# Batch 0's queries by parity of heads, landmarks of two batches ahead: a fused two-step attention and feed-forward kernel

## The chip, the core and the metric

The kernel runs on one core of a Trainium2 chip. A core has a matrix engine (TensorE, PE in the profile; its weight loads are PEld), a vector engine (VectorE, DVE), an engine for pointwise functions (ScalarE, ACT), GpSimd (POOL) and SyncE (SP). Each works through its own instructions in order and waits for the others on semaphores. Loads and stores are issued by SP and ACT (HWDGE, descriptors made in hardware) and by POOL (SWDGE, descriptors made by software, which can cast on the way); all share 16 DMA engines. The metric is the device time of one execution in microseconds, the median of several runs. The result is compared with a float32 reference.

## The reference

Eight batches of eight heads, 576 positions, width 64, with 32 landmarks p per head:

```
p_packed = softmax(scale * p k^T) v          # 32 x 64 per head
a        = softmax(scale * q p_packed^T) p_packed
x        = a, heads side by side             # 4608 tokens x 512
h        = x w_in                            # 4608 x 2048
g        = h if h >= 1;  0 if h <= -1;  (h + 1)^2 / 4 between
out      = g w_out                           # 4608 x 512
```

## The kernel before, in words

The kernel never forms x. For each batch it computes M = p_packed w_in (per head, so 8 x 32 = 256 rows by 2048 columns, kept as two groups g of 128 rows) and the normalized second softmax A (the same 256 rows by 576 tokens); then h = M^T A. Heads are paired: head 2a + g lies in group g, so group 0 has the even heads and group 1 the odd ones.

The stages of a batch, with their lines: turning the landmarks (`landmarks`, L321 on PE into tpp, copied by L189 into pT); turning k and q (`turned`, L362 into tp, copied into kT and qT); scores sp (L413) and their exponential ex (L419); p_packed and its row sums pk (L445, L450), copied into ppT, with reciprocals rs (L462); second scores s (L472, function `probs`, s2 in the code), exponential eT (L482), column sums sm (L487), logarithm ln (L491) and exponential rc (L495) for the reciprocal, product A (L500 on DVE); M (L528 into mp, in four slices f of 512 columns, each needing one slice of w_in, copied into M). Then 16 hidden blocks fi: h (L562, four products each), x (L567, ACT), t (L572 on DVE or L574 on ACT), hT (L579, DVE). The output (L619) is taken for pairs of batches in nine row blocks i of 128 tokens, each summing the 16 blocks fi; it needs w_out's slice fi // 4. L189 is the helper `copy`, through which all copies go.

The instructions are not in the order of the program text. Each step is added to a planner (`Plan`) with a rank, its duration on each engine that may do it, what it depends on and the buffers it takes. The planner runs through time with its own costs, picks for each engine the step of lowest rank among those that can start first, and so fixes engine and order; the program is then emitted in that order. The planner's ranks for batch 0's blocks, batch 1's stages and the first output blocks are the constants PITCH0, T1, L1, M1, KT1, QT1, SC1, ST1, MT1 and EARLY (start and length for each output block); LENT names output blocks of the first pair that take their accumulator from pool w instead of pool o. Pool w has three PSUM buffers, which serve every stage but the outputs; pool o has two.

Until the first output, PE's gaps are filled with products of zeros (L687, `warm`), as many as the planner's gaps hold; they keep PE active and compute nothing.

The loads go out by POOL in the order of the string LOADS (k0 is k of batch 0; heads 0 to 3 of it come by SP and ACT through k_raw, and the landmarks of batch 0 through p_raw, ahead of it on the same two queues). Batch 0's q comes in three parts of heads: 0 to 3, 4 and 5, 6 and 7. The landmarks of batches 1 to 7 (p) come by POOL behind k1. From batch 3 on, k and q are turned by DMA.

Of the kernel before, what the change touches and what calls it, by code (L numbers as in the profile page):

```python
# [116 lines left out]
def kernel(  # L117
# [35 lines left out]
    FIRST = 3  # L153
    LOADS = "k0 v0 q0 win0 win1 win2 wout0 win3 wout1 k1 p wout2 v1 wout3 q1 k2 q2 v2"
    H1, H2 = 20.58, 43.17
    PITCH0, PITCH1 = 1.03, 0.66
    T1, T2 = 3.46, 22.00
    LENT = [1, 4]
    L1, M1 = 11.28, 4.03
    KT1, QT1 = 7.75, 9.42  # L160
    SC1, PK1 = 10.26, 9.59
    ST1, MT1 = 12.34, 16.34
    EARLY = [[(3.62, 21.4), (13.89, 9.61), (23.95, 3.31), (31.73, 16.65)], [(26.33, 7.57), (43.04, 6.63), (54.6, 5.54), (55.23, 18.49), (62.39, 4.68)]]

# [31 lines left out]
    def either(dve, act, *pairs, parted=None):  # L196

        def emit(e):
            for to, of in pairs:
                copy(e, to(), of(), parted)  # L200
        return {"DVE": (dve[0], dve[1], emit), "ACT": (act[0], act[1], emit)}


    p_raw = const.tile([NP, H, D], f32, name="p_raw")
    p_nat = const.tile([NP, B, H, D], bf16)
# [12 lines left out]
    def constants(e):  # L218
        V.memset(zeros, 0.0)  # L219
        V.memset(pT[:, 0].rearrange("p g a x n -> p (g a x n)"), 0.0)  # L220
# [6 lines left out]
    consts = plan.add(-1000, {"DVE": (2.2, 2.2, constants)})  # L227

# [27 lines left out]
    def rows_of(nm, b, h0, h1):  # L256
        return {"k": k, "q": q, "v": v}[nm][b, h0:h1].rearrange("h (p c) d -> p h (c d)", c=NC)

    def load(nm, b, rank):

        parts = {("k", 0): [4, 8], ("q", 0): [0, 4, 6, 8]}.get((nm, b), [0, 8])
        for i, (h0, h1) in enumerate(zip(parts, parts[1:])):
            def emit(e, h0=h0, h1=h1):
                G_.dma_start(tokens(nm, b)[:, h0:h1], rows_of(nm, b, h0, h1))  # L264
            mb = MB0.get((nm, b, h0), 1.18 * (h1 - h0) / H)
            t = dma((nm, b, h0), rank + 0.01 * i, emit, mb, [nm] if i == 0 else [], 0.9 if b < FIRST else 3.0)
            for h in range(h0, h1):
                landed[nm, b, h] = [t]
# [8 lines left out]
    def load_p(rank):  # L277
        dma("p", rank, lambda e: G_.dma_start(p_nat[:, 1:].rearrange("n b h d -> n (b h) d"),
                                              p[1:].rearrange("b h n d -> n (b h) d")), 0.6)

# [13 lines left out]
    def load_p_raw(e):  # L294
        for i, queue in enumerate((nc.sync, nc.scalar)):
            queue.dma_start(p_raw[:, 4 * i:4 * i + 4], p[0, 4 * i:4 * i + 4].rearrange("h n d -> n h d"))

    p_first = plan.add(-1000, {"SP": (1.0, 3.3, load_p_raw)})

    def load_k_raw(e):  # L300
        for i, queue in enumerate((nc.sync, nc.scalar)):
            queue.dma_start(k_raw[:, 2 * i:2 * i + 2], rows_of("k", 0, 2 * i, 2 * i + 2))

# [32 lines left out]

    p_cast = plan.add(-900, {"DVE": (0.41, 0.41, lambda e: V.tensor_copy(p_nat[:, 0], p_raw))}, [p_first])
    landmarks(0, 1, -900, [p_cast, identity])

    A_of, M_of, rs_of = {}, {}, {}  # L340

    def attention(b, at, fine):

        ready = {}

        def turned(nm, h0, h1):

            n = h1 - h0
            rank = at[nm + "T"] + 0.075 * h0
            banks = [(0, (0, 2)), (1, (2, 3))] if n == 4 else [(j, (0, E)) for j in range(n)]  # L350

            def place(tp, j, c):
                return tp[:, 0, (j * 2 + c) * TP:][:, :TP] if n == 4 and c < 2 else \
                    tp[:, 1, j * TP:][:, :TP] if n == 4 else tp[:, j, c * TP:][:, :TP]

            def turn(e):
                if h0 == 0:
                    have[nm + "T", b] = new(nm + "T", [P, H, E, TP], bf16)
                have["tp" + nm, b, h0] = tp = wide([P, 2, 1024], bf16, "tp")
                for c in range(E):  # L360
                    for j in range(n):
                        nc.tensor.transpose(place(tp, j, c),  # L362
                                            have[nm, b][:, h0 + j, X * c:X * (c + 1)].rearrange("p c d -> p (c d)"),
                                            ident[:TP, :TP])

            t = plan.add(rank, {"PE": (0.51 * n / 4, 0.17 + 0.51 * n / 4, turn)}, landed[nm, b, h0] + [identity],
                         ["w"] + ([nm + "T"] if h0 == 0 else []), behind=[ready.get((nm, "turn"))])
            ready[nm, "turn"] = t
            ev = []
            for y, (c0, c1) in banks:  # L370
                to = lambda y=y, c0=c0, c1=c1: (have[nm + "T", b][:, h0:h1, c0:c1] if n == 4 else
                                                have[nm + "T", b][:, h0 + y])
# [8 lines left out]
            for h in range(h0, h1):  # L381
                ready[nm, h] = ev
            return t
# [13 lines left out]
        for nm in "kq":  # L397
            parts = [0, 4, 6, 8] if (nm, b) == ("q", 0) else [0, 4, 8]
            users[nm] = [turned(nm, *p) for p in zip(parts, parts[1:])] if b < FIRST else crossed(nm)
            plan.release(nm, users[nm])  # L400
# [29 lines left out]
        if b == 0:  # L430
            have["others"] = plan.add(-27, {"DVE": (1.56, 1.56, lambda e: V.memset(
                pT[:, 1:].rearrange("p b g a x n -> p (b g a x n)"), 0.0))}, [consts], behind=ready["k", 4])

# [31 lines left out]

        def probs(e):
            for g in range(G):
                have["s2", b, g] = s2 = wide([P, X, FW], f32, "s2")
                for a in range(Q):
                    for x in range(X):  # L470
                        r = slice(x * D, (x + 1) * D)
                        nc.tensor.matmul(s2[a * NP:(a + 1) * NP, x, :HALF], have["ppT", b][r, g, a],  # L472
                                         have["qT", b][r, G * a + g].rearrange("p e t -> p (e t)"),
                                         start=True, stop=True)

        s2 = plan.add(at["s2"], {"PE": (0.32, 0.47, probs)}, pp + list({id(t): t for h in range(H) for t in ready["q", h]}.values()), ["w", "w", "eT", "eT"], mode="s")
        plan.release("qT", [s2])
        before = None
        for g in range(G):
# [23 lines left out]
            r = at["sm"] + 0.2 * g  # L503
            t_e = plan.add(r, {"ACT": (0.68, 0.745, exp)}, [s2, rs])
            plan.release("w", [t_e])
# [13 lines left out]
        for fs in groups:  # L519
# [28 lines left out]
        plan.release("ppT", mms + [s2])  # L548

# [173 lines left out]
```

## Time and profile before

| | |
|---|---|
| median of 3 runs | 250.58 us (250.34 to 250.84) |
| the profiled execution | 250.97 us |
| its span, first to last instruction | 249.1 us |
| PE busy | 243.0 us, 98% of the span |
| ACT busy | 196.7 us, 79% |
| DVE busy | 176.6 us, 71% |
| filling products (L687) | 48, busy 13.5 us |
| loads and stores | 34.67 MB |

A row of the order of time gives start, duration, engine, line, operation, output and inputs, how often it stands there merged, and in brackets how long the engine had been idle and what ended that. The engine named is the one whose semaphore came last by the profile; where that engine had long been done, it was another, often a load. Rows of one engine overlap a little at their ends, since instructions are pipelined: four h products follow each other at shorter distance than the duration shown for each.

### The profile page before, as it was taken

The page shows a single profiled execution, that of the slowest core. Times are in us where ns is not written, and L with a number is a line of the kernel's source. Part 1 is how long each engine was busy: PE and PEld are TensorE (multiplying, and loading weights), DVE is VectorE, ACT ScalarE, POOL GpSimd, SP SyncE. Part 2 cuts the span into 40 slices and gives each one's busy share as a digit, 9 for nine tenths or more (in the row PEclk, how much of TensorE's full clock was granted, in tenths as well). Part 3 has the DMA queues.
Part 4 walks back from the last instruction along what each step waited for, and adds up shares of the span by engine and source line. Part 5 has one row for each costly group of instructions (what it writes and reads, how often), then busy time and mean ns, then how long its engine had stood idle before and what let it go on. Part 6 is the DMA issues. An engine that isn't in the chain of part 4 may idle for free.

```text
span 249.1 us, 5894 instructions
## 1 busy us (share of the span) xinstructions
PE 243.0 (98%) x2416; PEld 138.7 (56%) x2416; DVE 176.6 (71%) x295; ACT 196.7 (79%) x327; POOL 27.9 (11%) x41
## 2 busy tenths in 40 slices
PE   8999999999999999999999999999999999999994
PEld 3644665576645646645565455655565555555453
DVE  4548997679868999979966777679686776776000
ACT  4587986899799999899978977799968977886111
POOL 8542110211003000400030003000000000000000
PEclk9999999999999999999999999999999999999999
DMA  7999999999999949896999689995111111112223
GB/s 154 193 206 207 199 199 205 171 203 163 147 190 176 213 72 161 171 216 134 178 170 220 143 181 136 236 147 133 42 45 41 45 42 42 46 43 61 65 87 84
DMA packets 54508, 34.67 MB, mean 139 GB/s; under 512 B 27216, under 2 KB 50000, under 8 KB 54480
## 3 DMA queue, kind: packets, MB, share of 16 engines
q0 software_dynamic: 24496, 18.29, 49.6%
q1 hardware_dynamic: 29408, 15.47, 28.2%
q10 hardware_dynamic: 576, 0.52, 0.7%
q8 instruction: 19, 0.31, 0.5%
q14 instruction: 9, 0.07, 0.1%
HBM read 37.22 MB, written 9.44 MB: 187 GB/s over the span
## 4 chain that ended last, share of the span: by engine, by line
PE 90%; DMA 5%; ACT 2%; POOL 2%; issue 1%; DVE 0%; POOLq 0%
PE o L619 51%; PE h L562 24%; DMA w_in_sb<-in_moe_w_in_dram 5%; PE mp L528 4%; PE pk L445 2%; PE sp L413 2%; PE tp L362 2%; PE sm L487 1%; PE s L472 1%; PE pk L450 1%; PE o L687 1%; ACT x L567 1%; POOL q L264 1%; ACT M L189 0%; ACT ppT L189 0%
## 5 line engine op out<-in xcount | busy, mean ns | idle before, releaser
L619 PE MATMUL o<-w_out_sb,hT 128*128 128x512 bf16 (+1 forms) x592 | 149.9, 374 | 0.4 <-DVE t L572 0.4
L579 DVE SCALAR_TENSOR_TENSOR hT<-t 128x576 bf16<-128x576 f32 x128 | 95.5, 756 | 15.1 <-ACT t L574 12.3
L567 ACT ACTIVATE x<-h 128x576 f32<-128x576 f32 x128 | 80.8, 658 | 15.1 <-PE h L562 13.0
L619 PEld LDWEIGHTS <-hT 128*128 128x128 bf16 x592 | 56.1, 98 | 45.5 <-issue 5.0
L562 PE MATMUL h<-A,M 128*128 128x288 bf16 x512 | 80.8, 286 | 0.3 <-DVE rs L462 0.2
L562 PEld LDWEIGHTS <-M 128*128 128x128 bf16 x512 | 49.3, 98 | 30.5 <-issue 2.7
L572 DVE TENSOR_SCALAR t<-x 128x576 f32<-128x576 f32 x75 | 34.5, 460 | 14.7 <-ACT x L567 14.3
L574 ACT ACTIVATE t<-x 128x576 f32<-128x576 f32 x53 | 36.5, 691 | 1.1
L189 ACT COPY ob<-o 128x512 f32<-128x512 f32 (+1 forms) x20 | 11.3, 567 | 15.9 <-PE o L619 15.9
L189 ACT CAST M<-mp 128x1024 bf16<-128x1024 f32 (+1 forms) x22 | 21.3, 1004 | 1.4 <-PE mp L528 1.2
L264 POOL DMA_DIRECT2D q<-in_q_dram x10 | 7.6, 760 | 102.4 <-DMA qT<-q 78.8
L189 DVE CAST M<-mp 128x1024 bf16<-128x1024 f32 (+1 forms) x11 | 12.9, 1173 | 4.5 <-PE mp L528 4.5
L189 DVE COPY ob<-o 128x512 f32<-128x512 f32 x17 | 11.7, 690 | 5.8 <-PE o L619 5.4
L687 PE MATMUL o<-zeros 128*128 128x512 bf16 (+1 forms) x48 | 13.5, 408 | 1.2 <-DVE zeros L219 1.2
L419 ACT ACTIVATE ex<-sp 96x768 bf16<-96x768 f32 x16 | 12.7, 805 | 1.2 <-PE sp L413 1.1
L500 DVE SCALAR_TENSOR_TENSOR A<-eT,rs,rc 128x576 bf16<-128x576 bf16 x16 | 12.4, 813 | 0.8 <-ACT rc L495 0.8
L482 ACT ACTIVATE eT<-s,rs 128x576 bf16<-128x576 f32 x16 | 10.9, 734 | 1.8 <-PE s L472 1.3
L189 ACT CAST ppT<-pk 64x128 bf16<-64x128 f32 x24 | 6.2, 260 | 6.7 <-PE pk L450 6.3
L528 PE MATMUL mp<-w_in_sb,ppT 64*32 64x512 bf16 x256 | 10.4, 382 | 0.2 <-DMA w_in_sb<-in_moe_w_in_dram 0.2
L495 ACT ACTIVATE rc<-ln 128x576 f32<-128x576 f32 x16 | 10.2, 692 | 0.0
L491 ACT ACTIVATE ln<-sm 128x576 f32<-128x576 f32 x16 | 10.1, 656 | 0.1
L413 PEld LDWEIGHTS <-kT 128*128 128x128 bf16 x192 | 7.8, 100 | 3.5 <-issue 1.1
(47 smaller groups left out, 115.6 us busy)
## 6 DMA issues: line engine op xcount, KB each, us to landing
v<-in_v_dram POOLq DMA_DIRECT2D x8, 576.0 KB, 10.2
out_dram<-ob SPq DMA_DIRECT2D x23, 192.0 KB, 2.6
k<-in_k_dram POOLq DMA_DIRECT2D x7, 576.0 KB, 12.4
q<-in_q_dram POOLq DMA_DIRECT2D x7, 576.0 KB, 7.1
out_dram<-ob SPq DMA_DIRECT2D x24, 128.0 KB, 2.4
w_in_sb<-in_moe_w_in_dram POOLq DMA_DIRECT2D x4, 512.0 KB, 13.8
w_out_sb<-in_moe_w_out_dram POOLq DMA_DIRECT2D x4, 512.0 KB, 18.4
out_dram<-ob SPq DMA_DIRECT2D x23, 64.0 KB, 2.5
```

Of the source, the lines that this page charges most:

```text
L189: i = (nc.vector.tensor_copy if e == "DVE" else nc.scalar.copy)(to, of)
L413: nc.tensor.matmul(o, kT[:, j * TP:j * TP + w], pT[:, b, g, 2 * i + a], start=True, stop=True)
L419: nc.scalar.activation(have["ex", b][:, :, 64 * i:64 * i + 64], have["sp", b, i][:TP, :E * X * G], AF.Exp, scale=scale)
L500: V.scalar_tensor_tensor(have["A", b][:, g], have["eT", b, g], rs_of[b][:, g, :1], have["rc", b, g], ALU.mult, ALU.mult)
L528: nc.tensor.matmul(mp[a * NP:(a + 1) * NP, g], have["ppT", b][r, g, a], w_in_sb[r, a, f * FW:(f + 1) * FW], start=True, stop=True)
L562: nc.tensor.matmul(h[:, hf, :HALF], M[:, g, fi * P:(fi + 1) * P], A[:, g, hf], start=(g == 0), stop=(g == G - 1))
L567: nc.scalar.activation(x, have["h", b, fi][:, :, :HALF], AF.Prelu, bias=-1.0, alpha=0.5)
L572: V.tensor_scalar(t, have["x", b, fi], 1.0, 0.0, ALU.add, ALU.max)
L574: nc.scalar.activation(t, have["x", b, fi], AF.Relu, bias=1.0)
L579: V.scalar_tensor_tensor(dst, t, 1.0, t, ALU.min, ALU.mult)
L619: nc.tensor.matmul(have["o", key][:, :w], hT[:, fi, i * P:(i + 1) * P], w_out_sb[:, fi, cols], start=(fi == 0), stop=(fi == KF - 1))
L687: nc.tensor.matmul(o[:, :w], zeros[:, :P], zeros[:, :w], start=True, stop=True)
```

## The change

- Batch 0's q comes in the parts: even heads (0, 2, 4, 6), heads 1 and 3, heads 5 and 7. The functions that load and turn now take a list of heads with a step. The copy of the even heads' first PSUM bank is fixed to DVE and that of the second to ACT.
- In batch 0 the second scores are two units, one for each group g, each with its own buffers and dependences: group 0 needs the even heads and the first ppT copy alone.
- In batch 0 the first slice of M is copied in two halves as before, but the first half may only go to ACT, and the second is put behind the second product A.
- The landmarks of batches 0 and 1 come together at the start, batch 0 by SP and batch 1 by ACT, are cast and turned together; those of batches 2 to 7 come behind q1 and are turned in batch 2's place in the order. The zeroing of pT is divided accordingly.
- Most of the planner's constants named above have new values (PITCH0, T1, T2, L1, M1, KT1, QT1, SC1, MT1, EARLY), and output block 7 of the first pair also takes its accumulator from pool w.

```diff
+    Q0 = [range(0, 8, 2), range(1, 5, 2), range(5, 9, 2)]
-    LOADS = "k0 v0 q0 win0 win1 win2 wout0 win3 wout1 k1 p wout2 v1 wout3 q1 k2 q2 v2"
+    LOADS = "k0 v0 q0 win0 win1 win2 wout0 win3 wout1 k1 wout2 v1 wout3 q1 p k2 q2 v2"
-    PITCH0, PITCH1 = 1.03, 0.66
-    T1, T2 = 3.46, 22.00
-    LENT = [1, 4]
-    L1, M1 = 11.28, 4.03
+    PITCH0, PITCH1 = 1.11, 0.66
+    T1, T2 = 1.70, 18.09
+    LENT = [1, 4, 7]
+    L1, M1 = 18.22, 5.52
...
-    p_raw = const.tile([NP, H, D], f32, name="p_raw")
+    p_raw = const.tile([NP, 2, H, D], f32, name="p_raw")
...
-        dma("p", rank, lambda e: G_.dma_start(p_nat[:, 1:].rearrange("n b h d -> n (b h) d"),
-                                              p[1:].rearrange("b h n d -> n (b h) d")), 0.6)
+        dma("p", rank, lambda e: G_.dma_start(p_nat[:, 2:].rearrange("n b h d -> n (b h) d"),
+                                              p[2:].rearrange("b h n d -> n (b h) d")), 0.52)
...
-            queue.dma_start(p_raw[:, 4 * i:4 * i + 4], p[0, 4 * i:4 * i + 4].rearrange("h n d -> n h d"))
+            queue.dma_start(p_raw[:, i], p[i].rearrange("h n d -> n h d"))
...
-    p_cast = plan.add(-900, {"DVE": (0.41, 0.41, lambda e: V.tensor_copy(p_nat[:, 0], p_raw))}, [p_first])
-    landmarks(0, 1, -900, [p_cast, identity])
+    p_cast = plan.add(-900, {"DVE": (0.68, 0.68, lambda e: V.tensor_copy(p_nat[:, :2], p_raw))}, [p_first])
+    landmarks(0, 2, -900, [p_cast, identity])
...
+            if (nm, b, n) == ("q", 0, 4):
+                del ev[0].ways["ACT"], ev[1].ways["DVE"]
...
-        s2 = plan.add(at["s2"], {"PE": (0.32, 0.47, probs)}, pp + list({id(t): t for h in range(H) for t in ready["q", h]}.values()), ["w", "w", "eT", "eT"], mode="s")
-        plan.release("qT", [s2])
+        s2 = {}
+        for gs in [[0], [1]] if fine else [[0, 1]]:
+            needs = {id(t): t for g in gs for h in range(g, H, G) for t in ready["q", h]}
+            t = plan.add(at["s2"] + 0.01 * gs[0], {"PE": (0.08 + 0.12 * len(gs), 0.23 + 0.12 * len(gs), lambda e, gs=gs: probs(gs))},
+                         (pp if len(gs) > 1 else [pp[gs[0]]]) + list(needs.values()), ["w", "eT"] * len(gs), mode="s")
+            s2.update({g: t for g in gs})
...
                 ms = [plan.add(r + 0.01 + 0.3 * i, either(
...
-                    behind=[A_of[b][0]] if i else []) for i in range(n)]
+                    behind=[A_of[b][i]] if n > 1 and i else []) for i in range(n)]
+                if n > 1:
+                    del ms[0].ways["DVE"]
...
-        if b == 1:
-            landmarks(1, B, L1, [landed["p"], identity])
+        if b == 2:
+            landmarks(2, B, L1, [landed["p"], identity])
```

More of the change, by code (lines that the diff above doesn't have):

```diff
@@ L153 @@
     FIRST = 3
-    LOADS = "k0 v0 q0 win0 win1 win2 wout0 win3 wout1 k1 p wout2 v1 wout3 q1 k2 q2 v2"
+    Q0 = [range(0, 8, 2), range(1, 5, 2), range(5, 9, 2)]
+    LOADS = "k0 v0 q0 win0 win1 win2 wout0 win3 wout1 k1 wout2 v1 wout3 q1 p k2 q2 v2"
     H1, H2 = 20.58, 43.17
-    PITCH0, PITCH1 = 1.03, 0.66
-    T1, T2 = 3.46, 22.00
-    LENT = [1, 4]
-    L1, M1 = 11.28, 4.03
[L160 to L163, printed above, removed]
+    PITCH0, PITCH1 = 1.11, 0.66
+    T1, T2 = 1.70, 18.09
+    LENT = [1, 4, 7]
+    L1, M1 = 18.22, 5.52
+    KT1, QT1 = 7.69, 12.61
+    SC1, PK1 = 10.16, 9.59
+    ST1, MT1 = 12.34, 15.09
+    EARLY = [[(6.1, 22.07), (9.79, 10.57), (14.42, 1.45), (30.56, 17.66)], [(27.06, 2.62), (41.31, 8.4), (59.0, 3.81), (49.98, 14.33), (59.97, 2.94)]]
     V, A_, G_ = nc.vector, nc.scalar, nc.gpsimd
@@ L219, in constants @@
         V.memset(zeros, 0.0)
-        V.memset(pT[:, 0].rearrange("p g a x n -> p (g a x n)"), 0.0)
+        V.memset(pT[:, :2].rearrange("p b g a x n -> p (b g a x n)"), 0.0)
         V.memset(onesblk, 0.0)
@@ L225, in constants @@
         V.memset(ones2[:, 1:], 1.0 / scale)
-    consts = plan.add(-1000, {"DVE": (2.2, 2.2, constants)})
+    consts = plan.add(-1000, {"DVE": (2.4, 2.4, constants)})
     identity = plan.add(-998.5, {"POOL": (0.6, 1.25, lambda e: make_identity(nc, ident))})
@@ L254, in tokens, with heads, rows_of, emit @@
         return have[nm, b].rearrange("p h c d -> p h (c d)")
-    def rows_of(nm, b, h0, h1):
-        return {"k": k, "q": q, "v": v}[nm][b, h0:h1].rearrange("h (p c) d -> p h (c d)", c=NC)
+    def heads(hs):
+        return slice(hs[0], hs[-1] + 1, hs.step)
+    def rows_of(nm, b, hs):
+        return {"k": k, "q": q, "v": v}[nm][b, heads(hs)].rearrange("h (p c) d -> p h (c d)", c=NC)
     def load(nm, b, rank):
[L261 to L267, printed above, removed]
+        for i, hs in enumerate({("k", 0): [range(4, 8)], ("q", 0): Q0}.get((nm, b), [range(H)])):
+            def emit(e, hs=hs):
+                G_.dma_start(tokens(nm, b)[:, heads(hs)], rows_of(nm, b, hs))
+            mb = MB0.get((nm, b, hs[0]), 1.18 * len(hs) / H)
+            t = dma((nm, b, hs[0]), rank + 0.01 * i, emit, mb, [nm] if i == 0 else [], 0.9 if b < FIRST else 3.0)
+            for h in hs:
                 landed[nm, b, h] = [t]
@@ L301, in load_k_raw @@
         for i, queue in enumerate((nc.sync, nc.scalar)):
-            queue.dma_start(k_raw[:, 2 * i:2 * i + 2], rows_of("k", 0, 2 * i, 2 * i + 2))
+            queue.dma_start(k_raw[:, 2 * i:2 * i + 2], rows_of("k", 0, range(2 * i, 2 * i + 2)))
     k_first = plan.add(-999, {"SP": (1.0, 4.3, load_k_raw)}, behind=[p_first])
@@ L344, in attention, with turned @@
         ready = {}
-        def turned(nm, h0, h1):
-            n = h1 - h0
-            rank = at[nm + "T"] + 0.075 * h0
+        def turned(nm, hs, i):
+            n, h0 = len(hs), hs[0]
+            rank = at[nm + "T"] + 0.15 * i * (4 - n / 2)
             banks = [(0, (0, 2)), (1, (2, 3))] if n == 4 else [(j, (0, E)) for j in range(n)]
@@ L356, in turn @@
             def turn(e):
-                if h0 == 0:
+                if i == 0:
                     have[nm + "T", b] = new(nm + "T", [P, H, E, TP], bf16)
@@ L362, in turn @@
                         nc.tensor.transpose(place(tp, j, c),
-                                            have[nm, b][:, h0 + j, X * c:X * (c + 1)].rearrange("p c d -> p (c d)"),
+                                            have[nm, b][:, hs[j], X * c:X * (c + 1)].rearrange("p c d -> p (c d)"),
                                             ident[:TP, :TP])
             t = plan.add(rank, {"PE": (0.51 * n / 4, 0.17 + 0.51 * n / 4, turn)}, landed[nm, b, h0] + [identity],
-                         ["w"] + ([nm + "T"] if h0 == 0 else []), behind=[ready.get((nm, "turn"))])
+                         ["w"] + ([nm + "T"] if i == 0 else []), behind=[ready.get((nm, "turn"))])
             ready[nm, "turn"] = t
@@ L370, in turned @@
             for y, (c0, c1) in banks:
-                to = lambda y=y, c0=c0, c1=c1: (have[nm + "T", b][:, h0:h1, c0:c1] if n == 4 else
-                                                have[nm + "T", b][:, h0 + y])
+                to = lambda y=y, c0=c0, c1=c1: (have[nm + "T", b][:, heads(hs), c0:c1] if n == 4 else
+                                                have[nm + "T", b][:, hs[y]])
                 of = lambda y=y, c0=c0, c1=c1: (
@@ L379, in turned @@
                     parted=("tp" + nm, b, h0)), [t]))
+            if (nm, b, n) == ("q", 0, 4):
+                del ev[0].ways["ACT"], ev[1].ways["DVE"]
             plan.release("w", ev)
-            for h in range(h0, h1):
+            for h in hs:
                 ready[nm, h] = ev
@@ L397, in attention @@
         for nm in "kq":
-            parts = [0, 4, 6, 8] if (nm, b) == ("q", 0) else [0, 4, 8]
-            users[nm] = [turned(nm, *p) for p in zip(parts, parts[1:])] if b < FIRST else crossed(nm)
+            parts = Q0 if (nm, b) == ("q", 0) else [range(4), range(4, 8)]
+            users[nm] = [turned(nm, hs, i) for i, hs in enumerate(parts)] if b < FIRST else crossed(nm)
             plan.release(nm, users[nm])
@@ L430, in attention @@
         if b == 0:
-            have["others"] = plan.add(-27, {"DVE": (1.56, 1.56, lambda e: V.memset(
-                pT[:, 1:].rearrange("p b g a x n -> p (b g a x n)"), 0.0))}, [consts], behind=ready["k", 4])
+            have["others"] = plan.add(-27, {"DVE": (1.3, 1.3, lambda e: V.memset(
+                pT[:, 2:].rearrange("p b g a x n -> p (b g a x n)"), 0.0))}, [consts], behind=ready["k", 4])
         plan.release("kT", [scores(0), scores(1)])
@@ L464, in attention, with probs @@
         plan.release("w", pp + [rs])
-        def probs(e):
-            for g in range(G):
+        def probs(gs):
+            for g in gs:
                 have["s2", b, g] = s2 = wide([P, X, FW], f32, "s2")
@@ L474, in probs @@
                                          start=True, stop=True)
-        s2 = plan.add(at["s2"], {"PE": (0.32, 0.47, probs)}, pp + list({id(t): t for h in range(H) for t in ready["q", h]}.values()), ["w", "w", "eT", "eT"], mode="s")
-        plan.release("qT", [s2])
+        s2 = {}
[4 more added lines that the diff above has]
+            s2.update({g: t for g in gs})
+        plan.release("qT", list(set(s2.values())))
         before = None
@@ L503, in attention @@
             r = at["sm"] + 0.2 * g
-            t_e = plan.add(r, {"ACT": (0.68, 0.745, exp)}, [s2, rs])
+            t_e = plan.add(r, {"ACT": (0.68, 0.745, exp)}, [s2[g], rs])
             plan.release("w", [t_e])
@@ L547, in attention @@
                     M_of[b, Q * f + j] = ms[j * n // Q]
-        plan.release("ppT", mms + [s2])
+        plan.release("ppT", mms + list(set(s2.values())))
     g_of, h_of = {}, defaultdict(list)
```

## The prediction, made before the result was known

> **What bounds the kernel now.** I read the page's first line, then busy time by stretches, then the order of time on TensorE (PE), ScalarE (ACT) and VectorE (DVE) up to the first output product, and last the loads.
>
> ```profile
> span 249.1 us, 5894 instructions
> ```
>
> ```profile
> 19.30:24.80 5.50, 5.09 (x46) 2.88 (x45) 4.84 (x8) 4.39 (x8) 1.54 (x2) 1.00 1.24 207
> 24.80:66.00 41.20, 41.14 (x472) 25.38 (x472) 34.24 (x58) 34.84 (x60) 5.63 (x7) 1.00 1.17 184
> ```
>
> The columns are the stretch's length, then busy time (and instructions) of PE, its weight load, DVE, ACT, POOL, the granted clock (1.00), the loads' share and GB/s. PE seems nearly full in both stretches, but ahead of 24.8 us much of it is filling (products of zeros). From 24.8 to 66 PE stands 0.06 us out of 41.2, with real work. So the end is the time at which real work begins to fill PE, plus an amount of work that the change leaves alone (32 landmark transposes in both kernels, the same products). Only what PE gets done before 24.8, or a new stall behind it, can move the time.
>
> ```profile
> 13.16 0.43 PE L362 MATMUL tp<-ident,q 96*128 96x96 bf16 x6
> 13.43 0.71 PE L687 MATMUL o<-zeros 128*128 128x512 bf16 x3
> 14.06 0.44 PE L472 MATMUL s<-qT,ppT 64*32 64x288 bf16 x16
> ...
> 16.73 0.41 PE L528 MATMUL mp<-w_in_sb,ppT 64*32 64x512 bf16 x8 [0.23 <-DMA w_in_sb<-in_moe_w_in_dram]
> 17.07 2.33 PE L687 MATMUL o<-zeros 128*128 128x512 bf16 x10
> 19.33 0.41 PE L528 MATMUL mp<-w_in_sb,ppT 64*32 64x512 bf16 x8
> 19.68 1.16 PE L562 MATMUL h<-A,M 128*128 128x288 bf16 x8
> ...
> 23.77 0.65 PE L562 MATMUL h<-A,M 128*128 128x288 bf16 x4
> 24.84 0.59 PE L619 MATMUL o<-w_out_sb,hT 128*128 128x512 bf16 x2 [0.42 <-DVE t L572]
> ```
>
> ```profile
> 13.63 0.40 ACT L189 COPY qT<-tp 128x288 bf16<-128x288 bf16 x1 [0.50 <-PE tp L362]
> 14.46 1.37 ACT L482 ACTIVATE eT<-s,rs 128x576 bf16<-128x576 f32 x2 [0.43 <-PE s L472]
> 15.72 1.25 ACT L491 ACTIVATE ln<-sm 128x576 f32<-128x576 f32 x2
> 16.86 1.25 ACT L495 ACTIVATE rc<-ln 128x576 f32<-128x576 f32 x2
> 18.01 0.58 ACT L189 CAST M<-mp 128x512 bf16<-128x512 f32 x1
> 20.38 1.19 ACT L567 ACTIVATE x<-h 128x576 f32<-128x576 f32 x2 [1.79 <-PE h L562]
> ```
>
> ```profile
> 17.21 0.69 DVE L189 CAST M<-mp 128x512 bf16<-128x512 f32 x1 [3.27 <-PE mp L528]
> 17.82 1.54 DVE L500 SCALAR_TENSOR_TENSOR A<-eT,rs,rc 128x576 bf16<-128x576 bf16 x2
> ```
>
> The first output product waits at 24.84:
>
> ```profile
> 24.31 0.46 DVE L572 TENSOR_SCALAR t<-x 128x576 f32<-128x576 f32 x1
> ```
>
> The first three lists show the chain of batch 0: last q part, qT, s, eT, ln, rc, A (ready at 17.82 + 1.54 = 19.36), h. Beside it run the loads: w_in's first slice lets mp start at 16.73. For the wait at 24.84 the row names DVE's t, which ends at 24.77; but this product reads hT, whose first block was there long before, and the first slice of w_out:
>
> ```profile
> L275 POOL DMA_DIRECT2D w_out_sb<-in_moe_w_out_dram x4: 742/761/770, 7.6 to 21.9; - x4
> ...
> DMA to landing us min/median/max: 17.1/18.4/19.7
> ```
>
> Issued at 7.6 with the shortest landing of 17.1 (the loads behind it queue longer), that slice lands at 24.7. So I read the wait as the load's. That is a reading, and a rival below denies it.
>
> **Part 1: parity of heads, s2 in two units.** PE's order in the new build is: last six q transposes, s for g=0, one filling product, s for g=1. The first s unit needs the even heads alone, already turned, so it runs at about 13.6, beside the copies of the last q part. ACT does one of these (13.63 + 0.40 = 14.03), then starts eT at 14.03 instead of 14.46: 0.43 gained. eT, ln, rc stay back to back on ACT; in the row above they took 14.46 to 18.11, so now 17.68. The first half of M goes from DVE to ACT. DVE is then free when rc is: A began 0.32 late behind it (first rc about 17.5, A at 17.82). A's end becomes about 17.68 + 0.77 + 0.2 of pipe = 18.65 instead of 19.36, 0.71 gained. ACT pays a second M half, 0.58, and has both by 17.68 + 2 x 0.58 = 18.84; nothing waits for it there, since x was idle for 1.79 before 20.38. Were that cover gone it would cost its 0.58.
>
> **Part 2: h0 ahead of the second mp.** Before, mp stood first at 19.33 for its load, with h behind it at 19.68. Now the filling behind the first mp is 8 and a half products (10 took 2.33, so 1.81 to 1.98), ending near 18.9; h0 follows, then mp as its load allows. x begins at about 19.4 instead of 20.38: 0.97 earlier. Batch 0's chain through ACT and DVE is ahead by that when the first output is due.
>
> **What this is worth.** Before the first output the old kernel runs 24 h products (first row below: PE's products of that line up to 24.8), six blocks of four; the new order has 28, seven blocks. The second row, of the chain that ended last, prices a block:
>
> ```profile
> 0.00:24.80 24.80, 3.60 (x24) 2.26 (x24) 1.00 1.13 190
> ```
>
> ```profile
> 53.42 2.96 PE h L562 x24
> ```
>
> That is 2.96 / 6 = 0.49 us. If w_out's slice fixes the first output, the advance is cut to this one block, and the other 0.48 us of the 0.97 turns into waiting ahead of 24.8. Fewer filling products (43 for 48) give nothing by themselves: they stand in idle time.
>
> **Part 3: landmarks of two batches at the front.** Both HWDGE queues now carry 64 KB where each had 32 x 4 x 64 floats, 32 KB, ahead of k_raw: 64 KB more in all. First the load of the other landmarks, then loads and granted clock of two stretches:
>
> ```profile
> p_nat<-in_p_dram POOLq DMA_DIRECT2D x1, 224.0 KB, 20.0
> ```
>
> ```profile
> 1.50:3.00 1.50, 1.50 (x5) 0.58 (x4) 0.59 (x7) 0.53 (x1) 1.50 (x3) 1.00 0.58 139
> 30.50:32.00 1.50, 1.50 (x12) 0.98 (x10) 1.50 (x4) 1.50 (x4) 0.00 (x0) 1.00 2.19 167
> ```
>
> How far this pushes every load behind it, w_out's slice among them, is the unknown. Below: nothing, since from 1.5 to 3.0 the 16 engines were busy 0.58 of the time, which leaves 0.63 us of room. A gain is excluded: nothing ahead of w_out is removed. Above: 64 KB at that stretch's 139 GB/s, 0.47 us. I take 0.15, nearer the low end, because the extra packets run in just that stretch with room.
> [...]
>
> ```profile
> 2.81 0.55 DVE L337 CAST p_nat<-p_raw 32x512 bf16<-32x512 f32 x1 [0.69 <-DMA p_raw<-in_p_dram]
> ...
> 10.41 0.94 PE L445 MATMUL pk<-ex,v 96*64 96x32 bf16 x48
> ```
>
> The cast doubles to about 1.1, and the four landmark transposes become eight; with k_raw up to 0.47 late, k's transposes, scores and ex come 0.3 to 0.6 later. They are covered twice: pk waits for v until 10.41, and the q parts behind it fix 13.16. If both covers went, the whole 0.6 would appear.
>
> **Part 4: the other landmarks late.** p's 224 KB leave the place between k1 and w_out's third slice; at the 167 GB/s of the stretch in which its row peaks that is 1.4 us, by which w_out 2 and 3, v1 and q1 come sooner. PE was full there (0.06 us idle), so this earns nothing, and in exchange the landmark copies of six batches move from about 35.5 into batch 1's softmax:
>
> ```profile
> 35.54 1.81 ACT L189 COPY pT<-tpp 64x896 bf16<-64x896 bf16 x2 [0.31 <-PE tpp L321]
> ...
> 47.82 0.44 PE L472 MATMUL s<-qT,ppT 64*32 64x288 bf16 x16
> 48.19 0.68 PE L362 MATMUL tp<-ident,k 96*128 96x96 bf16 x12
> 48.71 0.60 PE L619 MATMUL o<-w_out_sb,hT 128*128 128x512 bf16 x2
> 49.15 0.41 PE L487 MATMUL sm<-eT,onesblk 128*128 128x288 bf16 x2
> ```
>
> On ACT, 1.81 x 6/7 = 1.55 now lies between qT and eT of batch 1. PE's sums wait for eT, and all of PE queues behind them. Before, 12 transposes and two outputs (about 0.96) stood between s and the sums; now six outputs and the transposes (6 x 0.22 + 0.52, about 1.8). I charge 0.05 net. POOL's queue: one issue moves past wout2, v1, wout3 and q1, which go out earlier; SP's gains nothing but p's larger issue.
>
> **Sum.** -0.49 (one block) + 0.15 (loads) + 0.05 (batch 1) = -0.29. The profiled execution is 250.97, of which 249.1 is the span; it is 0.39 above the median, 250.58. Carried to the median: 250.3.
>
> **Rivals.**
> Larger gain: the profile's row is right and the first output waited for DVE, not the load. Then the whole 0.97 shows: 250.58 - 0.97 + 0.15 = 249.8. For it: t ends at 24.77, 0.07 before PE starts. Against: hT's first blocks were done, and the landing at 24.7.
> Slower: the landmark copies hold up eT of batch 1. Uncovered, 1.55 less the added cover of 0.85 is 0.70 of PE standing still; it decides once p lands so late, or ACT arrives so late, that more than about 0.5 shows. With the full 0.47 push: 250.58 - 0.49 + 0.47 + 0.70 = 251.3. For it: PE runs in order and has no slack from 24.8 on. Against: q1 and p land about 1.4 sooner than q1 did.
> No effect: the push eats the block, 250.58 - 0.49 + 0.47 = 250.6.
>
> **Chances.** 0.2% is 0.5 us, about what a measurement of this kernel can tell from no change. My forecast 0.40, no effect 0.07, the larger gain 0.28, the slower case 0.25. The first two lie within 0.2%, though the forecast's upper half reaches past -0.5 when the push is nothing: faster 0.31, same 0.44, slower 0.25. The forecast's own range is 250.0 to 250.7; all cases but 2 in 10 lie in 249.6 to 251.3.
>
> **What would show it.** Right: eT near 14.1, h0 near 18.9 before the second mp, seven blocks before the first output, and that output still at 24.8 to 25.0. Wrong: the first output well before 24.7 (the larger gain); PE idle ahead of batch 1's sums around 48 us; w_in's first mp at 17.2 or later; or stalls between 25 and 33 us, where the third full M cast moves to ACT, which already is busy.

## The result and the profile after

The changed kernel takes 253.02 us (median of 6 runs, 252.27 to 255.82) against 250.38 us for the kernel before, measured beside it (6 runs, 250.23 to 250.84). The ratio is 1.0121, 95% interval 1.0095 to 1.0147: slower by 2.64 us between the medians. The profiled execution is the slowest of the six, 255.82 us with a span of 254.1; the reader should keep that in mind below, and the reason for it comes out of the profile.

The head of the page of the changed kernel, with the granted clock in 40 slices:

```profile
span 254.1 us, 5842 instructions
...
PEclk9999999977999999999999999999999999999999
```

In two slices, about 51 to 64 us, the clock granted to TensorE drops (mean 0.987 over the span); in the profile of before it does not (mean 1.000). First the front, from the order of time on PE (start, duration, engine, line, operation, and in brackets idle time and what ended it):

```profile
18.54 0.65 PE L576 MATMUL h<-A,M 128*128 128x288 bf16 x4
19.12 0.41 PE L539 MATMUL mp<-w_in_sb,ppT 64*32 64x512 bf16 x8
...
24.46 0.81 PE L633 MATMUL o<-w_out_sb,hT 128*128 128x512 bf16 x2 [0.34 <-DMA w_out_sb<-in_moe_w_out_dram]
```

The front and ACT (next list) do what was forecast: eT starts at 13.81 (14.46 before), the first h stands ahead of the second mp, x starts at 19.23 (20.38 before), and the first output waits for the first slice of w_out, which the profile now names itself.

```profile
13.81 1.38 ACT L493 ACTIVATE eT<-s,rs 128x576 bf16<-128x576 f32 x2
...
19.23 0.65 ACT L581 ACTIVATE x<-h 128x576 f32<-128x576 f32 x1 [0.79 <-PE h L576]
```

The loss stands at 51 us. PE's longest wait, then the place in the order of time:

```profile
PE tp L365 <- DMA q<-in_q_dram: 2.4, 1, 2.4
```

```profile
44.24 0.67 PE L365 MATMUL tp<-ident,q 96*128 96x96 bf16 x12
...
50.91 0.53 PE L419 MATMUL sp<-pT,kT 128*128 128x64 bf16 x12
53.79 1.14 PE L365 MATMUL tp<-ident,q 96*128 96x96 bf16 x12 [2.35 <-DMA q<-in_q_dram]
54.73 0.63 PE L633 MATMUL o<-w_out_sb,hT 128*128 128x512 bf16 x1
55.15 1.17 PE L365 MATMUL tp<-ident,q 96*128 96x96 bf16 x12
```

These are the query transposes of batch 2. The new order has them right behind batch 2's scores sp; the old order had them behind nine blocks h of batch 1, at 59.60. In the code their rank is T2 + 4 (T2 is the start of batch 2's stages), and T2 went from 22.00 to 18.09; no run changes T2 alone, but the run below that has all the old constants has the transposes behind nine blocks again. The issuing queue shows why they wait. First after, then before, then PE's order before:

```profile
45.21 0.77 POOL L267 DMA_DIRECT2D q<-in_q_dram  x1 [9.61 <-PE tp L365]
```

```profile
47.32 0.77 POOL L264 DMA_DIRECT2D q<-in_q_dram  x1 [11.54 <-PE o L619]
```

```profile
51.59 0.53 PE L413 MATMUL sp<-pT,kT 128*128 128x64 bf16 x12
...
53.26 3.13 PE L562 MATMUL h<-A,M 128*128 128x288 bf16 x24
...
59.60 0.68 PE L362 MATMUL tp<-ident,q 96*128 96x96 bf16 x12
```

There is one buffer for q. Batch 2's load can be issued only when batch 1's queries have been turned (44.24 + 0.67 = 44.91), and it lands near 53.8: 53.79 - 45.21 = 8.6 us. Before, 59.60 - 47.32 = 12.3 us lay between issue and use, and the load was hidden. After, PE reaches the place at 51.44 (50.91 + 0.53), 6.2 us behind the issue, and stands for 2.35. PE keeps a fixed order, so all that follows stands too.

Then the clock. Stretches of the changed kernel (length, busy time and instructions of PE, weight load, DVE, ACT, POOL, granted clock, share of the loads, GB/s):

```profile
51.30:53.80 2.50, 0.15 (x6) 0.04 (x2) 1.07 (x2) 1.25 (x2) 0.00 (x0) 0.94 1.17 209
53.80:54.60 0.80, 0.80 (x11) 0.80 (x12) 0.00 (x0) 0.00 (x0) 0.00 (x0) 0.50 1.31 244
54.60:60.00 5.40, 5.40 (x34) 3.60 (x32) 2.66 (x5) 2.60 (x5) 1.53 (x2) 0.50 1.20 173
60.00:61.00 1.00, 0.95 (x7) 0.66 (x7) 0.81 (x2) 0.76 (x2) 0.00 (x0) 0.84 1.25 183
```

The first stretch has 0.15 us of work in 2.5 us. Its mean clock, 0.94, puts the fall to 0.50 at about 53.5, still in the gap, and the mean of the last, 0.84, puts the return at about 60.3. From 53.8 on that is some 6.5 us of work at half clock, 3.2 us lost again, as the mean clock of this run says too (1 - 0.987, times 254.1, is 3.3). The six runs differ in this: at a mean clock of 1.00 they took 252.27, 252.61 and 252.68, at 0.998 253.36, at 0.993 254.64, at 0.987 255.82. A mean of 0.998 says little, since the kernel before has runs down to 0.997 (one of 249.96 us); what lifts the run of 253.36 is not shown. So the wait costs every run about 2 us, and the clock some 2 and 3.3 us more in two of the six.

The idle stretch was 2.35 us, and the clock fell, to 0.50, before it was over. What decides whether it falls in a run (it did in two of the six) is not shown.

### The profile page after: what moved, and what is told of

Read it like the earlier page. It is cut to its first block, busy times and chain, and to the rows that moved or that the text cites. A ratio compares the mean times of both kernels' runs of the same rounds, so it can differ in the third digit from the quotient of the medians.

```text
span 254.1 us, 5842 instructions
## 1 busy us (share of the span) xinstructions
PE 243.1 (96%) x2373; PEld 140.3 (55%) x2411; DVE 175.5 (69%) x295; ACT 197.9 (78%) x327; POOL 27.8 (11%) x41
## 4 chain that ended last, share of the span: by engine, by line
PE 84%; DMA 10%; POOL 2%; issue 2%; ACT 1%; DVE 0%; POOLq 0%
PE o L633 47%; PE h L576 24%; DMA w_out_sb<-in_moe_w_out_dram 7%; DMA q<-in_q_dram 3%; PE mp L539 3%; PE pk L451 2%; PE sp L419 2%; PE tp L365 2%; PE sm L498 1%; PE pk L456 1%; PE s L478 1%; POOL w_in_sb L274 1%; POOL q L267 1%; ACT ppT L190 0%; POOL v L267 0%
## 5 line engine op out<-in xcount | busy, mean ns | idle before, releaser
L633 PE MATMUL o<-w_out_sb,hT 128*128 128x512 bf16 (+1 forms) x557 | 142.1, 374 | 2.4 <-issue 0.6
L576 PE MATMUL h<-A,M 128*128 128x288 bf16 x512 | 82.3, 291 | 0.7 <-ACT x L581 0.3
L576 PEld LDWEIGHTS <-M 128*128 128x128 bf16 x512 | 49.9, 99 | 32.5 <-issue 4.3
L586 DVE TENSOR_SCALAR t<-x 128x576 f32<-128x576 f32 x78 | 36.0, 461 | 17.8 <-ACT x L581 17.5
L588 ACT ACTIVATE t<-x 128x576 f32<-128x576 f32 x50 | 34.4, 688 | 1.1
L190 ACT COPY ob<-o 128x512 f32<-128x512 f32 (+1 forms) x23 | 12.9, 571 | 16.0 <-PE o L633 15.9
L190 ACT CAST M<-mp 128x1024 bf16<-128x1024 f32 (+1 forms) x23 | 21.9, 987 | 2.2 <-PE mp L539 2.0
L190 DVE CAST M<-mp 128x1024 bf16<-128x1024 f32 x10 | 12.2, 1221 | 3.2 <-PE mp L539 3.2
L701 PE MATMUL o<-zeros 128*128 128x512 bf16 (+1 forms) x40 | 12.1, 420 | 1.4 <-DVE zeros L220 1.2
L190 DVE COPY ob<-o 128x512 f32<-128x512 f32 x14 | 9.7, 691 | 4.0 <-PE o L633 3.6
```

What stands on the lines that cost most here:

```text
L190: i = (nc.vector.tensor_copy if e == "DVE" else nc.scalar.copy)(to, of)
L576: nc.tensor.matmul(h[:, hf, :HALF], M[:, g, fi * P:(fi + 1) * P], A[:, g, hf], start=(g == 0), stop=(g == G - 1))
L586: V.tensor_scalar(t, have["x", b, fi], 1.0, 0.0, ALU.add, ALU.max)
L588: nc.scalar.activation(t, have["x", b, fi], AF.Relu, bias=1.0)
L633: nc.tensor.matmul(have["o", key][:, :w], hT[:, fi, i * P:(i + 1) * P], w_out_sb[:, fi, cols], start=(fi == 0), stop=(fi == KF - 1))
L701: nc.tensor.matmul(o[:, :w], zeros[:, :P], zeros[:, :w], start=True, stop=True)
```

## The experiments

**A buffer of its own for batch 2's queries.** The tile of k's first load is dead by then and has the right size, so batch 2's q goes there. No order is written differently.

```diff
-            have[nm, b] = new(nm, [TP, H, NC, D], bf16)
+            have[nm, b] = (k_raw.bitcast(bf16).rearrange("p a (h c d) -> p (a h) c d", h=2, c=NC)
+                           if (nm, b) == ("q", 2) else new(nm, [TP, H, NC, D], bf16))
```

> The changed kernel; batch 2's q gets its own memory (that of k_raw, dead by then), so its load no longer waits until batch 1's q has been turned. Order on every engine unchanged. Theory A (batch 2's q transposes stand too early in PE's order for a load that is issued only after batch 1's q is turned; PE then stands 2.35 us and the granted clock falls after it): PE's wait ahead of these transposes goes, the clock stays at 1.00, and the time is 249.7 to 250.1 us. Theory B (the loss comes from the front or from the landmarks' new place in the queue, and the wait for q only shows it): the time stays at 252 or more, PE waits elsewhere.

Measured: 250.97 us, ratio to the kernel before 1.0010 [0.9999, 1.0021]. The issue on POOL and the transposes on PE:

```profile
35.62 0.77 POOL L268 DMA_DIRECT2D k_raw<-in_q_dram  x1
```

```profile
51.37 0.68 PE L366 MATMUL tp<-ident,k_raw 96*128 96x96 bf16 x12
```

The load goes out at 35.62, nearly 10 us sooner, the wait is gone, and the mean clock stays at 0.998 to 1.00 in all twelve runs. That takes back 253.02 - 250.97 = 2.05 us of the 2.64 between the medians, and with the wait the runs above 253. But the time forecast for the rest, 249.7 to 250.1, was missed: without its wait the change is level with the kernel before (250.60 us beside it), not ahead of it.

**The transposes late again.** In the changed kernel, batch 2's query transposes are put behind block 8 of batch 1's h; one buffer, as in the change.

```diff
-                         ["w"] + ([nm + "T"] if i == 0 else []), behind=[ready.get((nm, "turn"))])
+                         ["w"] + ([nm + "T"] if i == 0 else []), behind=[ready.get((nm, "turn"))] + ([h_of[1][8]] if (nm, b) == ("q", 2) else []))
```

> The changed kernel; batch 2's q transposes may start only behind batch 1's hidden block 8, about where the kernel before has them; its load still waits as in the changed kernel. Theory A: 249.7 to 250.3 us, no wait ahead of the transposes, clock 1.00. Theory B: 252 or more.

Measured: 251.04 us, 1.0016 [1.0005, 1.0026], above the range expected, like the first experiment. A second way of covering the load gives the same: the transposes stand at 61.63 and no longer wait for the load (0.21 us, for DVE), so their move is the cause of the wait. PE's waits now list others, for batch 2's k and for the landmarks' turn:

```profile
PE tp L365 <- DMA k<-in_k_dram: 0.5, 1, 0.5
PE tpp L324 <- ACT qT L190: 0.5, 1, 0.5
```

**The wait filled with work.** Batch 2's second score unit runs its 12 products six times over, for nothing but time; the wait becomes products.

```diff
-                for c in range(E):
+                for c in [c for _ in range(6 if (b, i) == (2, 1) else 1) for c in range(E)]:
```

> The changed kernel; the 12 score products of batch 2's second unit are run six times over (the same values, five times for nothing), 2.2 us of PE work just ahead of the wait. Theory A: the wait shrinks to 0.2 us or less, the end stays where it is without a clock drop, 252.0 to 252.7 us in every run at clock 1.00; the runs above 253 vanish, since PE no longer idles long enough. If the clock drop has another cause, single runs still reach 253 to 256.

Measured: 252.95 us, 1.0085 [1.0072, 1.0099], a little above the 252.0 to 252.7 expected, and no run above 253.0.

```profile
51.37 2.36 PE L419 MATMUL sp<-pT,kT 128*128 128x64 bf16 x72
53.84 0.68 PE L365 MATMUL tp<-ident,q 96*128 96x96 bf16 x12
```

The transposes start where they did (53.84 for 53.79), but PE was busy until then, and the clock of this execution is 1.000. All six runs have a mean clock of 0.998 or more, with the order and the late load of the changed kernel. So the drop of the clock follows the idle time, not the load or the order. Six runs alone would leave some room for chance (if a third of the runs drop, six without a drop come about one time in eleven), but the fall inside the gap says the same. And 252.95 - 250.97 = 1.98 us is the price of the 2.35 us wait alone.

**The buffer alone.** The kernel before with the same two lines.

> The kernel before, with the same own memory for batch 2's q. Theory A: PE's transposes of that q stand behind nine hidden blocks there and do not wait, so nothing moves: 250.2 to 250.6 us. If the buffer itself were a gain in any order (an earlier load that relieves the queue), it would be 249.9 or less.

Measured: 250.48 us, 0.9999 [0.9990, 1.0007]. The buffer is worth nothing where the load was covered, so the first experiment measured the wait.

The next four stand on the first one and ask where the forecast gain went. The kernel before took 250.48 us beside these four and 250.60 beside the first, so the ratios to it compare better than the medians; the first had 1.0010 [0.9999, 1.0021].

**Batch 2's k ahead of the landmarks in the queue.**

```diff
-    LOADS = "k0 v0 q0 win0 win1 win2 wout0 win3 wout1 k1 wout2 v1 wout3 q1 p k2 q2 v2"
+    LOADS = "k0 v0 q0 win0 win1 win2 wout0 win3 wout1 k1 wout2 v1 wout3 q1 k2 p q2 v2"
```

> Built on the run with own memory for batch 2's q (median 250.97, 0.4 over the kernel before, where the prediction had 0.29 under it without that wait). Here k of batch 2 loads ahead of the late landmarks, which the planner then turns later. Theory C (what is left of the loss: PE, now ahead, meets k2 and the landmarks at about their landing, 44.8 to 48 us, and waits 0.3 to 1.0 in most executions): 250.1 to 250.5, no wait for k near 48. Theory D (the front part gains nothing in the first place): about 251.0 as before.

Measured: 252.56 us, 1.0084 [1.0070, 1.0098]. A miss for the theory that k's landing holds the gain: the wait only moved, to the landmarks and to batch 2's q, which here has k_raw's memory.

```profile
PE tpp L325 <- DMA p_nat<-in_p_dram: 1.0, 1, 1.0
PE tp L366 <- DMA k_raw<-in_q_dram: 0.8, 1, 0.8
```

**The front undone.** The old parts of q, s2 in one unit, M's halves free, in the changed kernel's stages.

```diff
-    Q0 = [range(0, 8, 2), range(1, 5, 2), range(5, 9, 2)]
+    Q0 = [range(0, 4), range(4, 6), range(6, 8)]
...
-        for gs in [[0], [1]] if fine else [[0, 1]]:
+        for gs in [[0, 1]]:
...
```

> On the run with own memory for batch 2's q, part 1 is undone: q of batch 0 in the parts 0 to 3, 4 and 5, 6 and 7, the second scores in one unit, M's first half free to go to DVE. The order of PE up to the first output is then that of the kernel before (six h blocks). Theory C: the front's 0.49 is lost but the later landings eat it anyway, 250.9 to 251.3. If the front part is worth its 0.49 at the end: 251.4 to 251.6. Theory D: 250.9 to 251.0.

Measured: 251.34 us, 1.0037 [1.0023, 1.0050], about 0.3 to 0.7 us above the first experiment and between the ranges expected. This looked like the forecast worth of the front. But the planner also reordered what follows (its trace waits 0.5 us for the landmarks), so it is no clean measure; the front alone, below, is.

**The landmarks of batches 2 to 7 at their old place in the queue.**

```diff
-    LOADS = "k0 v0 q0 win0 win1 win2 wout0 win3 wout1 k1 wout2 v1 wout3 q1 p k2 q2 v2"
+    LOADS = "k0 v0 q0 win0 win1 win2 wout0 win3 wout1 k1 p wout2 v1 wout3 q1 k2 q2 v2"
```

> On the run with own memory for batch 2's q, part 4 is undone: the landmarks of batches 2 to 7 load behind k1 again; PE's order is the same up to batch 1's packed product near 38 us. Theory C: v1, w_out 2 and 3 and q1 land 1.4 later again, PE meets q1 at its landing; batch 1's landmark copies leave its softmax: 250.5 to 251.0, no better than before. If the late landmarks are what costs the rest: 250.3 or less.

Measured: 250.96 us, 1.0025 [1.0015, 1.0035]. Within 0.01 us of the first experiment's median, and rather worse than better against the kernel before: loading them late is not what costs the rest. PE's order changes with the load here too, so what the late load earns, if anything, is not measured.

**w_out's first slice ahead of w_in's third.**

```diff
-    LOADS = "k0 v0 q0 win0 win1 win2 wout0 win3 wout1 k1 wout2 v1 wout3 q1 p k2 q2 v2"
+    LOADS = "k0 v0 q0 win0 win1 wout0 win2 win3 wout1 k1 wout2 v1 wout3 q1 p k2 q2 v2"
```

> On the run with own memory for batch 2's q, w_out's first slice loads ahead of w_in's third. If the first output waits for that slice (the reading in the prediction), it moves from 24.4 to about 22.3, where five blocks stand, PE fills 1 to 2 us earlier, and the time falls by 0.3 to 0.8: 250.2 to 250.7. If it waits for DVE (the rival), the first output stays near 24.4 and the time at 251.0.

Measured: 250.68 us, 1.0013 [1.0002, 1.0025]. From its order of time on PE:

```profile
22.77 0.38 PE L634 MATMUL o<-w_out_sb,hT 128*128 128x512 bf16 x1
...
28.82 1.20 PE L577 MATMUL h<-A,M 128*128 128x288 bf16 x8 [0.81 <-ACT M L190]
```

The first output comes 1.67 us sooner than in the first experiment (24.44), and hT's first block was there by then: the slice of w_out and its place in the order had pinned it, not DVE. Yet the median moves by only 0.3, and the ratio to the kernel before not at all (1.0013 for 1.0010); half of what was won stands at 28.82 as a wait for ACT's copy of M.

**The front alone, on the kernel before.** Parity of heads, s2 in two units and the halves of M; landmarks, loads and stages as before. From batch 1's second scores s on, PE's sequence is again that of the kernel before.

```diff
+    Q0 = [range(0, 8, 2), range(1, 5, 2), range(5, 9, 2)]
...
+        for gs in [[0], [1]] if fine else [[0, 1]]:
...
+                    behind=[A_of[b][i]] if n > 1 and i else []) for i in range(n)]
+                if n > 1:
+                    del ms[0].ways["DVE"]
```

> The kernel before with the front of the change alone: batch 0's queries by parity of heads, s2 in two units, the halves of M's first copy as in the change. The landmarks load as before, and the times and ranks of the stages are those of the kernel before, so TensorE has the kernel before's sequence again from batch 1's products s on, with batch 2's query transposes behind nine blocks h of batch 1. Theory A (the front is worth one block h, 0.5 to 0.7 us, and what the changed kernel lost beside the wait for q lies in its later sequence): 249.8 to 250.1 us, faster than before by 0.2% or more. Rival L (TensorE ahead by half a microsecond only meets the loads of batches 1 and 2 at their landing, whatever the sequence): 250.4 to 250.7, no difference from before, with waits for k, v or the landmarks of 0.3 us or more in the trace. Rival S (splitting s2 and loading by parity costs in itself): above 250.7.

Measured: 250.50 us, 1.0001 [0.9989, 1.0014]. No gain. Its first profiled execution took 250.16, that of the kernel before 250.97, with first outputs at 24.07 and 24.84, which would look like a gain. So both were profiled a second time, unchanged.

> The kernel before, unchanged, for a second profiled execution. The one that the forecast was worked from took 250.97 us, above the median of its runs. Reading F (the first output's time is fixed by the kernel and its loads, so the profile is typical): first output at 24.7 to 24.9 us, span less first output about 224.2 us, as in the first profile. Reading V (the front itself varies from one execution to the next by half a microsecond, because the loads land differently): first output anywhere from 24.1 to 24.9, and the time moves with it, the part behind it again 224.2 us.

> The front alone once more, for a second profiled execution; its first took 250.16 us with the first output at 24.07 us. Reading F: first output again at 24.1, 250.1 to 250.3 us. Reading V: first output anywhere from 24.0 to 24.8, the time moving with it, and the gain of 0.77 us at the first output of its first profile over that of the kernel before is in part the difference between two executions.

Measured: the kernel before 250.31 us with the first output at 24.08; the front alone 250.89 with the first output at 24.73. The front varies between executions, by about 0.7 us, in both kernels: the second reading was right. PE waits at the late ones (0.42 us at 24.84, 0.21 at 24.73) and not at the early ones. Products h of the two executions that have the first output at the same time (columns: length, then busy time and count of PE and of its weight load, clock, share of the loads, GB/s), first the kernel before, then the front alone:

```profile
0.00:24.05 24.05, 3.41 (x24) 2.25 (x24) 1.00 1.13 191
24.05:39.40 15.35, 6.56 (x42) 3.91 (x40) 1.00 1.39 201
```

```profile
0.00:24.05 24.05, 4.08 (x28) 2.56 (x28) 1.00 1.12 191
24.05:39.32 15.27, 5.91 (x38) 3.44 (x36) 1.00 1.39 201
```

The front alone has its seventh block, four products more, done ahead of the first output, and (by the weight loads, 36 for 40) one block fewer to do up to batch 1's pk. But it arrives there at 39.32 for 39.40. Where the block of 0.49 goes is in the order of time, again the kernel before and then the front alone:

```profile
26.72 0.41 PE L528 MATMUL mp<-w_in_sb,ppT 64*32 64x512 bf16 x8
...
28.77 0.65 PE L562 MATMUL h<-A,M 128*128 128x288 bf16 x4
...
39.40 0.93 PE L445 MATMUL pk<-ex,v 96*64 96x32 bf16 x48
...
47.50 0.68 PE L362 MATMUL tp<-ident,k 96*128 96x96 bf16 x12
```

```profile
27.14 0.41 PE L539 MATMUL mp<-w_in_sb,ppT 64*32 64x512 bf16 x8
...
28.68 0.65 PE L576 MATMUL h<-A,M 128*128 128x288 bf16 x4 [0.32 <-ACT M L190]
...
39.32 0.93 PE L451 MATMUL pk<-ex,v 96*64 96x32 bf16 x48
...
47.50 0.68 PE L365 MATMUL tp<-ident,k 96*128 96x96 bf16 x12
```

The fourth mp comes 0.42 later, because seven output products stand ahead of it in the new order and five in the old, and its copy, now on ACT, is not ready when the next h is due: 0.32 us of waiting, the larger part of the 0.49. At that h both kernels have done the same products, and the front alone is ahead by 0.09 (28.68 for 28.77). So the time is that of rival L, but the trace has the copy for its cause and not a load. By 47.50 the two kernels are level to the hundredth, and their spans are both 248.4. The other pair agrees: batch 2's first tp of k at 48.19 in the first profile of the kernel before and 48.21 in the second of the front alone, spans 249.1 both.

**The front alone, with w_out's first slice early.**

```diff
-    LOADS = "k0 v0 q0 win0 win1 win2 wout0 win3 wout1 k1 p wout2 v1 wout3 q1 k2 q2 v2"
+    LOADS = "k0 v0 q0 win0 win1 wout0 win2 win3 wout1 k1 p wout2 v1 wout3 q1 k2 q2 v2"
```

> The front of the change alone, as in the run before this one, and w_out's first slice loaded ahead of w_in's third. The first output should stand at 22.8 us in place of 24.4. If the time follows the first output: 249.5 to 249.9 us. If, as with w_out's slice first on the changed kernel, most of it goes into a wait for M's copies further on: 249.9 to 250.3. If loads set the time of batches 1 and 2 anyway: 250.4 to 250.8.

Measured: 251.92 us, 1.0053 [1.0039, 1.0067], with the first output at 22.52 and again 0.81 us of waiting for M, besides waits for w_out (0.3 us) and for copies (0.2 each) further on. All three times expected were missed: the first output came as early as expected, and the kernel is 1.4 us slower than the front alone, beside which it was measured. The waits are a part of that; the rest is not traced.

No kernel tried here beats the kernel before.

## Why the prediction was wrong

The forecast was 250.3 us, within 0.2% of before; it came to 253.02, outside the range.

*The step that failed* is the sentence that only what PE gets done before 24.8 "or a new stall behind it" can move the time, with Part 4's answer that there is no such stall but 0.05 in batch 1's softmax. Part 4 followed the landmarks alone; of POOL's queue it said that one issue moves past four others. The new values of the stage constants move batch 2's query transposes ahead of all of batch 1's h, and that was left out. What the runs put in its place: a wait of 2.35 us for a load that a single buffer holds back until batch 1's queries are turned, worth about 2 us (two ways of removing it give 250.97 and 251.04), and in two of the six runs some 2 and 3.3 us more through the clock, of which no run with work in the gap shows any. The trace of before held the numbers: q issued at 47.32 and used at 59.60, so 12.3 us of cover, of which the new order leaves 6.2.

*Part 1 and Part 2* were right in their times: eT 13.81 (forecast 14.03), A's end 18.49 (16.94 + 1.55; forecast 18.65, and 1.01 behind the end of rc, for 0.97 in the sum; the second A starts 0.19 behind that end, 17.67 for 17.48, where the sum has 0.2), h0 at 18.54 (18.9), x at 19.23 (19.4), seven blocks ahead of the first output.

```profile
16.94 1.55 DVE L511 SCALAR_TENSOR_TENSOR A<-eT,rs,rc 128x576 bf16<-128x576 bf16 x2 [3.11 <-ACT rc L506]
```

*What this is worth*, -0.49, was the second step that failed: the block is done sooner, but with the old order behind it the gain is about nothing (1.0001 [0.9989, 1.0014]). The text had named the place, "stalls between 25 and 33 us, where the third full M cast moves to ACT", among what would make it wrong, and had given it no price. In the changed kernel itself this M wait does not stand in the profile; there the remainder of 0.1% that is left without the q wait is not settled. The one trace of the first experiment is of its fastest run (250.25 us) and has 224.1 us from the first output to the end (248.5 - 24.44), 0.2 less than the kernel before; its slower runs, up to 251.50, have no trace. The traces of three relatives show PE waiting 0.3 to 0.5 us for batch 2's k, the landmarks or a copy near 45 to 49 us, but the run meant to prove that only traded one wait for others.

*The reading of the first output* as pinned by w_out's first slice was right for the two executions compared (the row at 24.46, and 22.77 with the slice first). It does not hold always: of the twelve executions with the slice in its old place, five show PE waiting there (0.21 to 0.46 us), and in seven PE comes to it, at 24.07 to 24.59, without a wait. The larger gain, by DVE, falls with the 22.77. *Part 3's* 0.15 for the extra 64 KB does not show: batch 0's pk starts at 10.30 to 10.78 in eight executions with them and at 10.41 to 10.75 in six without, 10.58 and 10.57 in the mean. The room of 0.63 us was no measure for it: the row beside it has a share of 2.19, so 1 is not the ceiling of that figure.

*The slower rival* had the sign but not the mechanism: batch 1's sums stand at 48.24 without a wait, and putting the landmark load back gained nothing. *No effect* is what came out for the front, though the loads did not eat the block; a copy took most of it.

*The base.* The sum was made against one execution, whose first output at 24.84 is the latest of the twelve; a second had 24.08, and the rest of the span was equal to 0.1 us. By these two traces the 0.39 us by which it stood above its median lies in the front and is not spread over the span.

## What to carry to other kernels

When an order changes, list for every load what frees its buffer and compare the time from that issue to the first use, before and after, with the landing time the trace shows; a load with 12 us of cover is not safe when its consumer moves 8 us forward (here 12.3 us became 6.2, and the load took 8.6). On an engine that is full, price an advance only after following it to the next copy or load it meets: here 0.49 us met M's copy, and 1.67 us did not become more than 0.3. The 2.35 us wait here was paid twice on TensorE in two of six runs: once as idle time, about 2 us, and once as a lower clock afterwards (0.50 for 6.8 us in the traced run), some 2 and 3.3 us.

## What the hardware showed that was not expected

A single 2.35 us wait came with a granted clock of 0.50 for 6.8 us in one execution (about 53.5 to 60.3) and a mean clock of 0.993 in another; the other four, at 0.998 to 1.00, show no more than runs of the kernel before do. With products in the gap none of six runs fell below 0.998, and the waits of 0.96 and 0.82 us in the run with k first left five runs at 0.998 or more. The same kernel has its first output at 24.08 in one execution and 24.84 in another, with the rest of the span equal to 0.1 us (224.32 and 224.26 from there to the end), so two profiles of two kernels can differ by 0.8 us for no reason of the kernels'.
